# One kernel, three layers: who loads the first row list, where the first weights stand, and which engine makes the late rows' low parts

## The chip, the cores and the metric

The kernel runs on one core of a Trainium2 chip. The core has TensorE (PE, matmuls), VectorE (DVE), ScalarE (ACT), GpSimd (POOL) and SyncE (SP). DMAs are issued from the queues of SP, ACT and POOL; each queue is worked off in order. The metric is the device time of one execution in microseconds (us); three runs before the change gave 816.40, 819.06 and 818.17, median 818.17.

## The reference, cut to what matters

```python
scores = (q @ k.T) / 8                      # batch 4, 8 heads, 576 rows, head size 64
masks: heads 0-3 a local band of 32, heads 4-7 causal rows with equal position mod 32
x = softmax(where(mask, scores, -1e9)) @ v  # -> x: 2304 rows of 512
logits = x @ w_gate; e = argmax(logits)     # one of 8 experts for each row
gate = softmax(logits)[e]; eom = sigmoid((x @ w_output_gate)[e])
y = gate * eom * (relu(x @ w1[e]) @ w2[e])  # 512 -> 1024 -> 512, by expert
h = relu(y @ w_in); out = (h * h) @ w_out   # 512 -> 2048 -> 512
```

## The kernel before, in words

Three stages follow one another. Attention works batch by batch through units: a score product, softmax, a transposition, the product with v (`unit`, `unit2`, `unit3`). When all units that 128 rows need are done, `gates` makes the row tile `xr` of these rows: a product `rw` turns x over and gives the gate logits beside it, `lg` sums the logits, and SP stores the rows to the table `x_d` in DRAM. There are 18 such tiles in four groups (4, 5, 4 and 5 tiles). After a group `route` finds each row's expert (`mx`, `d`, `oh`) and its place in the expert's list (a product `rk`, then `posi`), and POOL scatters the row numbers into `tab_d`, one indirect DMA for each tile.

Second stage: the experts, largest first, 416 rows for the first. The rows of an expert are gathered from `x_d` by its list. All products are made in three parts: an operand is split into a high part (`hw`, `xh`, `xa`; ACT) and a low part (`lw`, `xl`, `xb`; a subtraction), and high x high, high x low and low x high are summed in PSUM (`mm3`). Third stage: the dense layers, on products of smaller blocks.

The place of the change is the end of attention. After group 2 (tiles 9 to 12) `largest` picks the expert that the first 13 tiles fill most, `e0`. `early_load` then loads its list `ix` from `tab_d`, two pieces of its first weights (`r`, 512 KB each) and gathers its rows (`win`, four blocks of up to 128). `first_rows` turns the first 208 of them over on PE (`wt`) and copies the others into two accumulators `lr`. The rows of the last five tiles (13 to 17) are not gathered: `late_rows` multiplies their parts `xa` and `xb` by 0/1 matrices `pm`, which put each row at its place in `lr`. Then comes the first product `h` of the expert.

A scheduler with modelled times decides the order on each engine, within the order of the program for each tile's data; `tc.issue_after` sets an instruction behind another one. Queues are first in, first out, so an instruction that waits holds up all behind it on its engine. Tile buffers: `xr` has four (`XRB`), so tile 17 takes the buffer of tile 13 after its store and its `xa` and `xb`; `raw`, `wh` and `wl` hold the weights. Names at work: L491 `xb`, L516 `ix`, L520 `win`, L534 and L538 `e0` and `r`, L587 and L596 `wt` and `lr`, L622 `lr` from `pm`, L703 the scatters, L915 and L919 `hw` and `lw`.

Of the kernel before, what the change touches and what calls it, by code (L numbers as in the profile page):

```python
# [7 lines left out]
F32 = mybir.dt.float32  # L8
# [5 lines left out]
ALU = mybir.AluOpType  # L14
# [6 lines left out]
P = 128  # L21
# [39 lines left out]
HB = 8  # L61

MG = [(3, 3), (3, 3), (3, 3)]
LPOOL = (13, 14, 15, 16, 17)
DS = 6
LN = 6
FILL = (2, 3)
PMB = 5
LWP = 0

# [61 lines left out]
def moe_kernel(ctx, tc, q, k, v, wg, wog, w1, w2, w_in64, w_out64, consts, out, dbg=None):  # L132
# [335 lines left out]
    def gates():  # L468
        while gq and needs(gq[0][1]) <= done:
            g, t = gq.pop(0)  # L470
            t0, t1 = GROUPS[g]
            if t == t0:
                xrs[g] = wk.tile([P, 5, 2 * E], F32, name=f"lg{g}", tag="lg", bufs=2), []
            lg, rows = xrs[g]
            xr = wk.tile([P, KD, W], F32, name=f"xr{t}", tag="xr", bufs=XRB)
            col = t * P % (2 * S)
            for kh in range(2):
                ps = pss.tile([P, 2, W], F32, name=f"rw{t}_{kh}", tag=TAILT.get((t, kh), "tp"))
                for kk in range(2):
                    kd = kh * 2 + kk  # L480
                    nc.tensor.matmul(ps[:, kk, :], xT[:, kd, col : col + P], igw[:, kd, :], start=True, stop=True)  # L481
                evac(xr[:, 2 * kh : 2 * kh + 2, :], ps)
            nc.vector.tensor_reduce(
                lg[:, t - t0, :], xr[:, :, P:].rearrange("p k c -> p c k"), axis=AX.X, op=ALU.add
            )
            rows.append(xr)
            if t >= LATE:
                parts[t] = xa, xb = [wk.tile([P, KD, P], F32R, name=f"x{i}{t}", tag="xp", bufs=XPB) for i in "ab"]
                nc.scalar.activation(xa, xr[:, :, :P], AF.Copy)
                eng = nc.gpsimd if t in LPOOL else nc.vector  # L490
                eng.tensor_tensor(xb, xr[:, :, :P], xa.bitcast(F32), op=ALU.subtract)  # L491
            stq(x_d[1 + t * P : 1 + (t + 1) * P, :], xr[:, :, :P])
            if t == t1 - 1:
                route(g, list(range(t0, t1)), lg, rows)
                if t1 == LATE:
                    lead["do"] = largest
                elif t0 >= LATE:
                    late_rows(t0, t1, rows)

    def stq(dst, src):  # L500
        nc.sync.dma_start(dst.rearrange("p (k c) -> p k c", c=P), src)
# [8 lines left out]

    tab_e = tab_d.rearrange("(e r) o -> e (r o)", e=E)

    def rows_of(k, reg):
        ix = const.tile([P, NW], I32, name=f"ix{k}")
        nw = (CAPS[k] + P - 1) // P
        nc.sync.dma_start(ix[:, :nw], tab_e[bass.ds(reg, 1), : nw * P].rearrange("e (c p) -> p (e c)", p=P))  # L516
        return ix

    def gather(out_, ix, n=1 + NT):
# [7 lines left out]
    def win_get(k, r, ix, n=1 + NT):  # L527
        m = min(P, CAPS[k] - r)
        wins[k, r // P] = w = early[0].tile([P, KD, P], F32, name=f"win{k}_{r}", tag="win", bufs=4)
        lead["win"] = gather(w[:m].rearrange("p k c -> p (k c)"), ix[:m, r // P : r // P + 1], n)  # L530

    def early_load():
        e0 = lead["e0"]
        oreg[0] = nc.values_load(e0[0:1, :], engines=[ET.SP], min_val=0, max_val=E - 1)  # L534
        lead["ix"] = rows_of(0, oreg[0])
        for c in range(2):
            raw = early[0].tile([P, KD, UC], F32, name=f"r0_{c}", tag="raw", bufs=2)
            nc.sync.dma_start(  # L538
                raw, w1[bass.ds(oreg[0], 1), :, c * UC : (c + 1) * UC].rearrange("e (a p) f -> p (e a) f", p=P)
            )  # L540
            eraw["w1", 0, c] = raw

        for r in range(0, CAPS[0], P):
            win_get(0, r, lead["ix"], 1 + LATE * P)

    def largest():

# [26 lines left out]
    def first_rows():  # L574

        xh = early[0].tile([P, KD, CAPS[0]], F32R, name="xh0", tag="xh")
        xl = early[0].tile([P, KD, CAPS[0]], F32R, name="xl0", tag="xl")
        xsp[0] = (xh, xl)
        acc["p"] = [pss.tile([P, 2, NL], F32, name=f"lr{h}", tag="pt") for h in range(2)]
        for t in range((CAPS[0] + P - 1) // P):  # L580
            R = min(P, CAPS[0] - t * P)
            w = wins[0, t]
            c = max(0, min(R, C0 - t * P))
            if c:
                ps = pss.tile([P, KD, P], F32, name=f"wt0_{t}", tag=("o", "os")[t % 2], bufs=1)
                for a in range(KD):
                    nc.tensor.transpose(ps[:, a, :c], w[:c, a, :], ident[:c, :c])  # L587
                cs = slice(t * P, t * P + c)
                nc.scalar.activation(xh[:, :, cs], ps[:, :, :c], AF.Copy)
                with tc.issue_after(lead["pm"].ins):  # L590
                    nc.vector.tensor_tensor(xl[:, :, cs], ps[:, :, :c], xh[:, :, cs].bitcast(F32), op=ALU.subtract)
            if c < R:
                cs = slice(t * P + c - C0, t * P + R - C0)
                with tc.issue_after(lead["rk"].ins) if t in FILL else nullcontext():
                    for a in range(KD):
                        nc.tensor.matmul(  # L596
                            acc["p"][a // 2][:, a % 2, cs],
                            w[:R, a, :],
                            ident[:R, c:R],
                            start=(t == C0 // P and a % 2 == 0),  # L600
                            stop=False,
                        )

    def late_rows(t0, t1, rows):
        rel = wk.tile([P, 5], F32, name=f"rel{t0}", tag="rel")
        nc.vector.tensor_scalar(rel[:, : t1 - t0], posi[:, t0:t1], lead["base"], None, op0=ALU.subtract)
        pms = []
        for t in range(t0, t1):
            pm = wk.tile([P, NL], F32R, name=f"pm{t}", tag="pm", bufs=PMB)
            lead["pm"] = nc.vector.tensor_scalar(  # L610
                pm, cst[:, C_IO : C_IO + NL], rel[:, t - t0 : t - t0 + 1], None, op0=ALU.is_equal
            )
            pms.append((t, pm))
        if t0 == LATE:
            first_rows()
        xh, xl = xsp[0]
        for h in range(2):
            ps = acc["p"][h]
            for t, pm in pms:
                for a in range(2):  # L620
                    for x in range(2):
                        nc.tensor.matmul(  # L622
                            ps[:, a, :],
                            parts[t][x][:, 2 * h + a, :],
                            pm,
                            start=False,
                            stop=(t == NTILE - 1 and a == x == 1),
                        )
            if t1 == NTILE:
                to = (slice(None), slice(2 * h, 2 * h + 2), slice(C0, CAPS[0]))  # L630
                nc.scalar.activation(xh[to], ps, AF.Copy)
                lead["last"] = nc.vector.tensor_tensor(xl[to], ps, xh[to].bitcast(F32), op=ALU.subtract)  # L632
# [94 lines left out]
    for b in range(B):  # L727
        t = tiles[b]
        tn = transposes(b + 1, tiles[b + 1]) if b + 1 < B else iter(())
        for n, ku in enumerate(ORDER[b].split()):  # L730
            next(tg, None)
            kind, u = ku[0], int(ku[1:])
            q2.append((b, t, kind, u) + unit(b, t, kind, u))
            drain(D2, D3)
            if b == B - 1 and n >= LN and "do" in lead:
                lead.pop("do")()
                lead["ok"] = 1
            if b == B - 1 and not early and all(a[0] == b for a in q2 + q3):
                front.close()
                early.append(  # L740
                    bulk.enter_context(tc.tile_pool(name="early", bufs=1, side="right", reuse_waits="tile"))
                )
            if scq and nun[0] >= scq[0][0] and (b < B - 1 or "ok" in lead):
                with tc.issue_after(last_ev["p"].ins):
                    scq.pop(0)[1]()
            if n >= (5 if b == 0 else 1):
                next(tn, None)
                if b == 0:
                    next(tn, None)
        for _ in tn:  # L750
            pass
        tg = iter(())
        if b + 2 < B:
            tiles[b + 2] = load(b + 2)
# [112 lines left out]
    def prep_unit(u):  # L867
# [43 lines left out]
        pool, nb = (raws, 2) if nwh[0] % WB < 2 else (mp, WB - 2)  # L911
        hi = pool.tile(shp, F32R, name="h" + nm, tag="wh", bufs=nb)
        first = u in eraw
        with tc.issue_after(last_ev["s"].ins) if first else nullcontext():
            nc.scalar.activation(hi, raw, AF.Copy)  # L915
        lo = pool.tile(shp, F32R, name="l" + nm, tag="wl", bufs=nb)
        eng = nc.gpsimd if first and LWP else nc.vector
# [472 lines left out]
```

## Time and profile before

| | us |
|---|---|
| median of three runs | 818.17 |
| the profiled execution | 815.72 |
| its span in the trace | 813.9 |
| PE busy | 763.5 (94%) |
| DVE busy | 553.9 (68%) |
| ACT busy | 493.3 (61%) |
| POOL busy | 216.8 (27%) |

The page gives the busy time of each engine, the span in 40 slices of 20.3 us, and the chain that ended last: for each piece of work what released it. The trace behind it is read by timelines (instructions in order, with the idle time before them and what ended it), by stretches (windows) and by tiles. Times below count from the span's start. An SP or POOL row of a DMA is its issue; the transfer lands later.

### The profile page before, as it was taken

Reading aid. Unit: us, or ns where it says so; the run is one execution under the profiler, and the core shown is the slowest. Engines: PE = TensorE matmul, PEld = TensorE weight load, DVE = VectorE, ACT = ScalarE, POOL = GpSimd, SP = SyncE. Lnnn points to the kernel's source line nnn. Section 1 sums busy time; section 2 is a strip of 40 time slices with the busy share of each in tenths; the row PEclk is TensorE's granted clock in tenths of the full one; section 3 lists DMA queues with packets and bytes.
Section 4 is the critical chain, followed back from the end, with each engine's and each line's share of the span. In section 5 each row is a group of like instructions: output and inputs, shape, how many; then the busy total and the mean of one; then the engine's idle time right before and its main releaser. Section 6 shows DMA issues by size and latency. Waiting matters only on the chain.

```text
span 813.9 us, 14424 instructions
## 1 busy us (share of the span) xinstructions
PE 763.5 (94%) x5139; PEld 704.9 (87%) x5139; DVE 553.9 (68%) x1109; ACT 493.3 (61%) x1197; POOL 216.8 (27%) x210
## 2 busy tenths in 40 slices
PE   4999799599999999999989999999999999999993
PEld 3988789599999999999978888888889988888893
DVE  4778578565467578779889777787654687566442
ACT  2878588524455465656677676766655586556542
POOL 7223133537065764431133121004000003000002
PEclk9999989779999999999999999999999999999998
DMA  8987801629679999876554633524232235223002
GB/s 175 201 178 136 189 21 54 191 63 333 202 188 267 196 303 283 298 258 210 172 195 147 218 128 123 175 91 149 91 118 77 76 105 182 72 87 102 1 1 81
DMA packets 106691, 124.85 MB, mean 153 GB/s; under 512 B 42801, under 2 KB 77137, under 8 KB 106610
## 3 DMA queue, kind: packets, MB, share of 16 engines
q1 hardware_dynamic: 97026, 100.77, 43.6%
q0 software_dynamic: 8096, 22.63, 8.6%
q8 instruction: 42, 0.69, 0.4%
q10 hardware_dynamic: 1488, 0.44, 0.3%
q14 instruction: 39, 0.32, 0.2%
HBM read 101.70 MB, written 22.12 MB: 152 GB/s over the span
## 4 chain that ended last, share of the span: by engine, by line
PE 55%; issue 17%; DMA 9%; DVE 7%; ACT 6%; POOL 4%; SPq 1%; POOLq 0%; ACTq 0%; DVEq 0%
DMA s0wo<-in_moe_w_out_dram 4%; PE o L935 4%; PE h L935 4%; PE o L936 4%; PE o L937 4%; PE y L935 4%; PE y L936 3%; PE h L936 3%; PE y L937 3%; PE h L937 3%; PE rw L481 2%; DMA ks<-in_k_dram 1%; DMA rw<-in_moe_w_dram 1%; POOL win L520 1%; PE lr L622 1%
## 5 line engine op out<-in xcount | busy, mean ns | idle before, releaser
L935 PE MATMUL o<-hwo,gh 128*128 128x512 f32 x288 | 114.2, 397 | 3.8 <-ACT gh L1063 3.8
L936 PE MATMUL o<-lwo,gh 128*128 128x512 f32 x288 | 113.4, 394 | 0.0
L919 DVE TENSOR_TENSOR lw<-rw,hw 128x1024 fp32r<-128x1024 f32 x62 | 78.2, 1262 | 43.2 <-ACT hw L915 42.6
L1149 ACT ACTIVATE rl<-rl 128x384 f32<-128x384 f32 x96 | 49.5, 519 | 94.9 <-DVE rl L1147 94.8
L915 ACT ACTIVATE hw<-rw 128x1024 fp32r<-128x1024 f32 x62 | 65.9, 1062 | 65.2 <-PE h L936 44.9
L1176 POOL DMA_INDIRECT out_dram<-ob,idx x18 | 20.6, 1147 | 275.5 <-ACT ob L1175 271.0
L1064 DVE TENSOR_TENSOR gl<-rl,gh 128x384 fp32r<-128x384 f32 x96 | 56.8, 593 | 44.3 <-ACT gh L1063 43.2
L937 PE MATMUL o<-hwo,gl 128*128 128x512 f32 x288 | 83.6, 396 | 2.0 <-DVE gl L1064 2.0
L935 PE MATMUL h<-xh,hw 128*128 128x416 f32 (+7 forms) x256 | 81.0, 316 | 1.6 <-DVE hl L1035 1.5
L937 PE MATMUL h<-xh,lw 128*128 128x416 f32 (+7 forms) x256 | 79.5, 310 | 0.0
L936 PE MATMUL h<-xl,hw 128*128 128x416 f32 (+7 forms) x256 | 79.5, 310 | 0.0
L936 PE MATMUL y<-hl,hw 128*128 128x416 f32 (+7 forms) x256 | 77.1, 310 | 0.0
L937 PE MATMUL y<-hh,lw 128*128 128x416 f32 (+7 forms) x256 | 76.6, 310 | 0.0
L935 PE MATMUL y<-hh,hw 128*128 128x416 f32 (+7 forms) x256 | 68.0, 311 | 0.4 <-ACT hh L1034 0.4
L935 PEld LDWEIGHTS o<-hwo,gh 128*128 128x128 f32 x288 | 54.0, 188 | 15.5 <-ACT gh L1063 6.3
L937 PEld LDWEIGHTS o<-hwo,gl 128*128 128x128 f32 x288 | 53.6, 188 | 12.8 <-DVE gl L1064 3.0
L936 PEld LDWEIGHTS o<-lwo,gh 128*128 128x128 f32 x288 | 54.1, 188 | 9.0
L1063 ACT ACTIVATE gh<-rl 128x384 fp32r<-128x384 f32 x96 | 49.9, 521 | 1.8
L935 PEld LDWEIGHTS h<-xh,hw 128*128 128x128 f32 x256 | 48.1, 188 | 3.1 <-DVE hl L1035 2.9
L1150 ACT ACTIVATE rl<-rl 128x384 f32<-128x384 f32 x96 | 49.6, 519 | 1.7
L936 PEld LDWEIGHTS h<-xl,hw 128*128 128x128 f32 x256 | 48.2, 188 | 0.3 <-DVE xl L632 0.2
L936 PEld LDWEIGHTS y<-hl,hw 128*128 128x128 f32 x256 | 48.1, 188 | 0.1
(602 smaller groups left out, 2066.6 us busy)
## 6 DMA issues: line engine op xcount, KB each, us to landing
rw<-in_moe_w_dram SPq DMA_DIRECT2D x62, 512.0 KB
rwa<-ws_d SPq DMA_DIRECT2D x24, 512.0 KB
rwb<-ws_d SPq DMA_DIRECT2D x24, 384.0 KB
e6wi<-in_moe_w_in_dram SPq DMA_DIRECT2D x32, 256.0 KB
rwo<-wout_d SPq DMA_DIRECT2D x16, 512.0 KB
x_d<-xr SPq DMA_DIRECT2D x18, 256.0 KB
ws_d<-eo POOLq DMA_DIRECT2D x16, 256.0 KB, 5.1
s0wo<-in_moe_w_out_dram SPq DMA_DIRECT2D x8, 512.0 KB
```

Source lines behind the costliest of these rows:

```text
L481: nc.tensor.matmul(ps[:, kk, :], xT[:, kd, col : col + P], igw[:, kd, :], start=True, stop=True)
L520: return nc.gpsimd.indirect_dma_start(out=out_, out_offset=None, in_=x_d[:n, :], in_offset=bass.IndirectOffsetOnAxis(ap=ix, axis=0),)
L915: nc.scalar.activation(hi, raw, AF.Copy)
L919: eng.tensor_tensor(lo, raw, hi.bitcast(F32), op=ALU.subtract)
L935: nc.tensor.matmul(ps, ah, bh, start=first, stop=False)
L936: nc.tensor.matmul(ps, ah, bl_, start=False, stop=False)
L937: nc.tensor.matmul(ps, al, bh, start=False, stop=last)
L1063: nc.scalar.activation(h, x, AF.Copy)
L1064: nc.vector.tensor_tensor(l, x, h.bitcast(F32), op=ALU.subtract)
L1149: nc.scalar.activation(rl[:, :HC], src, AF.Relu)
L1150: nc.scalar.activation(rl[:, :HC], rl[:, :HC], AF.Square)
L1176: ins = nc.gpsimd.indirect_dma_start(out=out[:, :], out_offset=bass.IndirectOffsetOnAxis(ap=idx[:, gt_, 0:1], axis=0), in_=ob, in_offset=None,
```

## The change

Seven edits. (1) The list `ix` is loaded from POOL's queue, right ahead of the gathers, and no longer from SP's; e0's value is read on POOL for it. (2) The loads of `r` become `first_weights`, called behind the store of tile 15. (3) The high parts `hw` of `r` are issued behind the last `xa`. (4) All `xb` are made on DVE; that of tile 17 behind the last `pm`. (5) `LN`, the first unit of the last batch at which `largest` may run, is 4 and was 6, and up to two scatters are issued at a step of the last batch. (6) All row transpositions and copies are issued behind `rk`. (7) `late_rows` runs its loops by half, part, tile.

```diff
-LPOOL = (13, 14, 15, 16, 17)
-LN = 6
-FILL = (2, 3)
+LN = 4
@@ gates
-                nc.scalar.activation(xa, xr[:, :, :P], AF.Copy)
-                eng = nc.gpsimd if t in LPOOL else nc.vector
-                eng.tensor_tensor(xb, xr[:, :, :P], xa.bitcast(F32), op=ALU.subtract)
+                lead["xa"] = nc.scalar.activation(xa, xr[:, :, :P], AF.Copy)
+                lead["xb"] = lambda: nc.vector.tensor_tensor(xb, xr[:, :, :P], xa.bitcast(F32), op=ALU.subtract)
+                if t < NTILE - 1:
+                    lead["xb"]()
             stq(x_d[1 + t * P : 1 + (t + 1) * P, :], xr[:, :, :P])
+            if t == NTILE - 3:
+                first_weights()
@@ rows_of, early_load
-    def rows_of(k, reg):
+    def rows_of(k, reg, eng=nc.sync):
-        nc.sync.dma_start(ix[:, :nw], tab_e[bass.ds(reg, 1), : nw * P].rearrange("e (c p) -> p (e c)", p=P))
+        eng.dma_start(ix[:, :nw], tab_e[bass.ds(reg, 1), : nw * P].rearrange("e (c p) -> p (e c)", p=P))
     def early_load():
         e0 = lead["e0"]
-        oreg[0] = nc.values_load(e0[0:1, :], engines=[ET.SP], min_val=0, max_val=E - 1)
-        lead["ix"] = rows_of(0, oreg[0])
+        e0p = nc.values_load(e0[0:1, :], engines=[ET.Pool], min_val=0, max_val=E - 1)
+        lead["ix"] = rows_of(0, e0p, nc.gpsimd)
+        for r in range(0, CAPS[0], P):
+            win_get(0, r, lead["ix"], 1 + LATE * P)
+    def first_weights():
+        oreg[0] = nc.values_load(lead["e0"][0:1, :], engines=[ET.SP], min_val=0, max_val=E - 1)
         for c in range(2):
...
@@ first_rows
-                for a in range(KD):
-                    nc.tensor.transpose(ps[:, a, :c], w[:c, a, :], ident[:c, :c])
+                with tc.issue_after(lead["rk"].ins):
+                    for a in range(KD):
+                        nc.tensor.transpose(ps[:, a, :c], w[:c, a, :], ident[:c, :c])
-                with tc.issue_after(lead["rk"].ins) if t in FILL else nullcontext():
+                with tc.issue_after(lead["rk"].ins):
@@ late_rows
+        if t1 == NTILE:
+            with tc.issue_after(lead["pm"].ins):
+                lead["xb"]()
-            for t, pm in pms:
-                for a in range(2):
-                    for x in range(2):
+            for x in range(2):
+                for t, pm in pms:
+                    for a in range(2):
@@ the loop over units
-                with tc.issue_after(last_ev["p"].ins):
-                    scq.pop(0)[1]()
+                for _ in range(2 if b == B - 1 else 1):
+                    if scq and nun[0] >= scq[0][0]:
+                        with tc.issue_after(last_ev["p"].ins):
+                            scq.pop(0)[1]()
@@ prep_unit
-        with tc.issue_after(last_ev["s"].ins) if first else nullcontext():
+        with tc.issue_after(lead["xa"].ins) if first else nullcontext():
             nc.scalar.activation(hi, raw, AF.Copy)
```

POOL at attention's end, before; `tab_d<-tok_92` is a scatter (the first is tile 8's), and the waits name the semaphores of DMA queues and engines:

```order
L372 TENSOR_TENSOR pr3s_2130<-pr3s_2130,rc3s_2137 72x4x72 [waits DVE_49,PE_49,Activation_49]
L372 TENSOR_TENSOR pr3s_2194<-pr3s_2194,rc3s_2201 72x4x72 [waits DVE_49,PE_49,Activation_49]
L372 TENSOR_TENSOR pr3s_2224<-pr3s_2224,rc3s_2231 72x4x72 [waits DVE_49,PE_49,Activation_49]
L703 DMA tab_d<-tok_92,posi 18432x1 [waits DMASW0_49]
L703 DMA tab_d<-tok_92,posi 18432x1 [waits DMASW1_49,DVE_49]
...
L703 DMA tab_d<-tok_92,posi 18432x1 [waits DMASW4_49]
L520 DMA win_0_2405<-x_d,ix_2399 128x512 [waits DMAHW4_49,DMAHW3_49,DMAHW5_49,DMAHW2_49,DMAHW6_49,DMAHW1_49,DMAHW7_49,DMAHW0_49,DMASW5_49]
...
L520 DMA win_384_2411<-x_d,ix_2399 32x512 [waits DMASW0_49]
L491 TENSOR_TENSOR xb_2482<-xr_2471,xa_2481 128x512 [waits DVE_49,Activation_49]
```

The same place now:

```order
L370 TENSOR_TENSOR pr3s_2130<-pr3s_2130,rc3s_2137 72x4x72 [waits DVE_49,PE_49,Activation_49]
L713 DMA tab_d<-tok_92,posi 18432x1 [waits DMASW0_49]
L370 TENSOR_TENSOR pr3s_2212<-pr3s_2212,rc3s_2219 72x4x72 [waits DVE_49,PE_49,Activation_49]
L370 TENSOR_TENSOR pr3s_2244<-pr3s_2244,rc3s_2251 72x4x72 [waits DVE_49,PE_49,Activation_49]
L713 DMA tab_d<-tok_92,posi 18432x1 [waits DMASW1_49,DVE_49]
...
L713 DMA tab_d<-tok_92,posi 18432x1 [waits DMASW4_49]
L536 TENSOR_LOAD e_2196 [waits DVE_49]
...
L517 DMA ix_2281<-tab_d 128x4x1 [waits DMASW5_49,DMASW4_49]
L521 DMA win_0_2283<-x_d,ix_2281 128x512 [waits DMAHW3_49,DMAHW4_49,DMAHW2_49,DMAHW5_49,DMAHW1_49,DMAHW6_49,DMAHW0_49,DMAHW7_49,DMASW6_49,DMASW5_49]
...
L521 DMA win_384_2289<-x_d,ix_2281 32x512 [waits DMASW1_49]
L713 DMA tab_d<-tok_92,posi 18432x1 [waits DMASW2_49,DVE_49]
```

The list stands between the last scatter of group 2 and the gathers, `xb` is gone, and tile 8's scatter moved ahead of two `pr3s`.

SP behind the store of tile 12, before (`r0_0` and `r0_1` are `r`):

```order
L501 DMA x_d_82<-xr12_2072 512x1x128 [waits DMAHW3_49,DVE_49,Activation_49]
L534 TENSOR_LOAD e0_2260 [waits DVE_49]
L534 ISA x2
L516 ISA
L516 DMA ix0_2399<-tab_d_83 128x4x1 [waits DMAHW4_49,DMASW4_49]
L538 ISA
L538 DMA r0_0_2401<-in_moe_w1_dram 128x4x256 [waits DMAHW5_49,PE_49]
L538 ISA
L538 DMA r0_1_2403<-in_moe_w1_dram 128x4x256 [waits DMAHW6_49]
L501 DMA x_d_82<-xr13_2471 512x1x128 [waits DMAHW7_49,DVE_49,Activation_49]
```

And now:

```order
L502 DMA x_d_82<-xr12_2072 512x1x128 [waits DMAHW3_49,DVE_49,Activation_49]
L543 TENSOR_LOAD e0_2196 [waits DVE_49]
L543 ISA x2
L546 ISA
L546 DMA r0_0_2554<-in_moe_w1_dram 128x4x256 [waits DMAHW4_49,PE_49]
L546 ISA
L546 DMA r0_1_2556<-in_moe_w1_dram 128x4x256 [waits DMAHW5_49]
L502 DMA x_d_82<-xr13_2467 512x1x128 [waits DMAHW6_49,DVE_49,Activation_49]
```

Only the list's two rows are gone from SP; `r` still stands behind tile 12's store and ahead of tile 13's.

## Rows read from the trace of the kernel before

**Rows 1.** The page, 40 slices: PE busy and granted clock, in tenths.

```profile
PE   4999799599999999999989999999999999999993
PEclk9999989779999999999999999999999999999998
```

**Rows 2.** PE timeline, end of the late products: start us, us, what.

```profile
173.62 0.28 PE L622 MATMUL lr<-pm,xb 128*128 128x208 f32 x1
173.73 0.37 PE L935 MATMUL h<-xh,hw 128*128 128x416 f32 x1
```

**Rows 3.** PE timeline, 149 to 168 us; idle time before it in brackets.

```profile
149.32 2.23 PE L481 MATMUL rw<-igw,xT 128*128 128x144 f32 x16 [0.53 <-DVE xT L270]
157.15 1.08 PE L587 MATMUL wt<-cst,win 128*128 128x128 f32 x4 [5.61 <-DMA win<-x_d,ix]
...
158.99 1.86 PE L596 MATMUL lr<-cst,win 128*128 128x48 f32 x8
163.10 0.22 PE L655 MATMUL rk<-oh,cstb 128*128 128x40 bf16 x1 [2.26 <-DVE oh L652]
...
163.53 3.92 PE L596 MATMUL lr<-cst,win 128*128 128x128 f32 x16
...
167.43 0.52 PE L622 MATMUL lr<-pm,xa 128*128 128x208 f32 x1
```

**Rows 4.** The chain that ended last, 142 to 151 us: start, us, what.

```profile
141.95 6.18 DMA tab_d<-tok,posi
148.15 2.16 DMA ix<-tab_d
```

**Rows 5.** SP's queue, issues, 148 to 159 us.

```profile
148.82 0.97 SPq L538 DMA_DIRECT2D r<-in_moe_w_dram  x2
149.91 8.54 SPq L501 DMA_DIRECT2D x_d<-xr  x5
```

**Rows 6.** POOL timeline, 131 to 163 us.

```profile
131.03 0.66 POOL L372 TENSOR_TENSOR pr3s<-pr3s,rc3s 72x288 f32<-72x288 f32 x1 [2.64 <-DVE lg L483]
...
151.39 0.99 POOL L520 DMA_INDIRECT win<-x_d,ix  x1 [8.21 <-issue]
...
155.21 0.88 POOL L520 DMA_INDIRECT win<-x_d,ix  x1 [0.30 <-issue]
156.11 6.17 POOL L491 TENSOR_TENSOR xb<-xr,xa 128x512 fp32r<-128x512 f32 x5
```

**Rows 7.** ACT timeline, the first split of r.

```profile
153.43 1.06 ACT L915 ACTIVATE hw<-r 128x1024 fp32r<-128x1024 f32 x1 [4.78 <-DMA r<-in_moe_w_dram]
```

**Rows 8.** DVE timeline, routing of the last five tiles.

```profile
157.43 0.46 DVE L270 COPY xr<-rw 128x288 f32<-128x288 f32 x1 [6.37 <-POOL xb L491]
...
158.28 0.20 DVE L638 TENSOR_REDUCE mx<-lg 128x5 f32<-128x40 f32 x1
158.51 3.83 DVE L640 TENSOR_TENSOR d<-lg,mx 128x40 f32<-128x40 f32 x1
...
164.37 1.31 DVE L610 TENSOR_SCALAR pm<-cst,rel 128x208 fp32r<-128x208 f32 x5
```

**Rows 9.** Tile ix, SP: ns min/median/max, first and last start us.

```profile
L516 SPq MOVE ix<-tab_d x8: 29/29/38, 141.5 to 320.9; - x8
```

**Rows 10.** DVE timeline, low parts of r.

```profile
166.60 2.34 DVE L919 TENSOR_TENSOR lw<-r,hw 128x1024 fp32r<-128x1024 f32 x2
```

**Rows 11.** Tile tab_d: scatters from issue to landing.

```profile
DMA to landing us min/median/max: 2.8/5.8/12.9
```

**Rows 12.** Windows: us, busy of PE, PEld, DVE, ACT, POOL, clock, DMA, GB/s.

```profile
150.00:155.00 5.00, 1.54 (x13) 1.33 (x11) 0.46 (x1) 1.13 (x2) 2.90 (x3) 0.91 1.05 287
...
165.00:170.00 5.00, 5.00 (x24) 4.71 (x24) 3.94 (x7) 0.00 (x0) 4.01 (x4) 0.50 0.10 27
```

**Rows 13.** The page's DMA issues: KB each, median us to landing.

```profile
idx<-idx_d POOLq DMA_DIRECT2D x1, 18.0 KB, 6.9
```

**Rows 14.** Tile win: gathers from issue to landing.

```profile
DMA to landing us min/median/max: 3.3/5.7/8.7
```

More of the change, by code (lines that the diff above doesn't have):

```diff
@@ L541, in early_load @@
             eraw["w1", 0, c] = raw
-        for r in range(0, CAPS[0], P):
-            win_get(0, r, lead["ix"], 1 + LATE * P)
     def largest():
```

## The prediction

> **What bounds the kernel now.** I read the slices of the page first. TensorE (PE) is near nine tenths or more in most of them; one slice in the middle, the eighth, falls to 5 while the granted clock sinks to 7 in it and in the next [rows 1]. That slice lies at 142 to 163 us, attention's end, where the first expert's rows are fetched. After it PE is full to the last slices, so I take a microsecond saved here as a microsecond of the end, and a time in this stage is told by one event: the first matmul of the first expert, h, at 173.73 us [rows 2].
>
> Second, PE's own timeline [rows 3]. The last routing products rw begin at 149.32 and end at 151.55. Then PE idles 5.61 us for the gathered rows (win). From 157.15 to 160.85 it turns the first two blocks over and copies a part of the second into the sums (wt, first lr): 3.70 us. Then it idles 2.26 us for oh, VectorE's one-hot of the last five tiles, and ranks it (rk, 0.43 us). The other blocks (lr from win) take 163.53 to 167.38, 3.85 us, and the 40 products with the late tiles (lr from pm) 167.43 to 173.73, 6.30 us. So two chains meet on PE: rows, then oh; the later one is oh.
>
> Third, what each chain waits for. Rows: the last scatter of row numbers is issued at 141.95 and has landed 6.18 us later; the list is loaded (ix) in 2.16 us [rows 4]; SP issues it at 148.15, and the weights r and five x_d stores stand behind it [rows 5]; GpSimd (POOL) starts the first gather at 151.39 [rows 6], 1.08 us after the list landed at 150.31; the block is on PE 5.76 us after that [rows 3]. oh: ScalarE (ACT) sits 4.78 us waiting for the late weights, and copies of late rows stand behind that in its queue [rows 7]; VectorE (DVE) waits 6.37 us for POOL's xb to free a buffer, copies at 157.43, and its subtraction d then takes 3.83 us beside xb instead of 0.20 us, as mx ahead of it took on the same few numbers [rows 8]. POOL's five xb run from 156.11 to 162.28, and d ends just behind them, at 162.34 [rows 6, 8].
>
> **The change part by part.** *Weights, weight splits, xb (the oh chain).* In the order SP no longer holds the list, so r leaves at about 141.5, when SP had set the list's address, for which it needs the same e0 [rows 9], and the stores behind it leave as their rows are ready. ACT's splits of r move behind the last xa, so no late row waits for it. Four xb go to DVE before the routing, one behind pm. A DVE subtraction on twice as many elements is 1.17 us (2.34 for two) [rows 10], so one xb is about 0.6 us by that row, the four together 2.4 us. I bound that at 0 (all beside waits for PE, which DVE has there) and 2.4. The buffer that tile 17 takes over is then free, and its store gone, before the product ends at 151.55; its copy comes at about 152, where before it was 157.43: 5.4 us earlier, and d costs 0.2 in place of 3.83, so 3.6 more. pm, done at 165.68 [rows 8], would be done at 165.68 - 5.4 - 3.6 = 156.7, at the latest 159.1 with all xb in front. PE needs pm only after all rows from win, far later. Behind pm DVE now has the last xb and r's two lw before the first blocks' xl: 156.7 + 0.6 + 2.3 = 159.6, about when PE has turned the first block over, so xl loses nothing. On POOL the last five scatters follow the gathers some 7 us earlier; nobody waits for them sooner. The oh chain is off the path, and none of its 9.0 us counts by itself.
>
> *What is late next: the list on POOL.* The rows chain now sets PE alone, and here the change has costs.
> - Scatter. Its landing gates the list as before. r now runs beside it, where before SP stood waiting. All scatters land in 2.8 to 12.9 us [rows 11]; this one in 6.18. Ends: -3.4 and +6.7 us. r's 1 MB at the 287 GB/s of the full stretch [rows 12] is through in 3.7 us, by about 145, before the old landing, so I take +0.7.
> - List transfer. Before, 2.16 us through SP. In the trace no list goes through POOL. The nearest rows: 2.8, the fastest scatter (128 pieces) [rows 11], and 6.9, the table idx with 2,304 pieces of 8 bytes [rows 13]. The list is 512 pieces of 4 bytes; on the line between the two that is 2.8 + 384/2176 x 4.1 = 3.5 us, and I take it. Ends: 2.16 and 6.9.
> - List to gather. Before 1.08 us, with eight further semaphores named behind the list's; now the list's is named last, and I take 0.3, the gap between two gathers. Ends 0.3 and 1.08.
> - Gather to PE: 5.76 kept (x_d and later weights still load the queues). Ends 3.3 and 8.7, all gathers [rows 14].
> - Rows on PE: 3.70 + 3.85 in one piece now, since rk is done before, at the low clock: 7.55. The fourth gather starts 3.8 us after the first, before its turn on PE 5.7 us after the first block.
> - Late products: the same 40, ordered by half and part, so 6.30 if the clock returns as far behind their start as before. The last of them, at the full clock, start 0.11 us apart [rows 2]; at the half clock that is 0.22: ends 40 x 0.11 = 4.4 and 40 x 0.22 = 8.8.
>
> The sum: 148.15 + 0.7 + 3.5 + 0.3 + 5.76 + 7.55 + 6.30 = 172.3, against 173.73: 1.4 us gained. The count (cntp) moves behind the products for 0.05 us, nothing.
>
> *The Trainium skill on the list.* On the rows a POOL transfer costs more than SP's (2.8 and up against 2.16). The Trainium skill, DMA: Bandwidth & Descriptors, section Latency and other measured facts, puts the first byte at some 0.6 us by hardware descriptors and 1 us by GpSimd's: only 0.4 apart. By it the list would take an estimated 2.56 us and h start at 171.3, 2.4 us gained.
>
> *LN, two scatters a step.* Only one scatter moves in POOL's order, tile 8's, ahead of two products pr3s. It takes 1 us where POOL idled 2.64 us before the first of them [rows 6]; if that cover were gone, pr3s would be 1 us later, a small loss. The last scatter still waits for the ranks on DVE, so it isn't earlier. *Transposes behind rk* cost nothing: rk would come at about 154, before the first block at 158.4.
>
> **Rivals.**
> *1. The clock returns earlier.* PE's row work is now one unbroken run into the late products. If the clock rises before these, they take 4.4 instead of 6.3: gain 3.3 us. Against it: before, PE worked from 163.53 without a gap and was still at a granted 0.50, 1.2 GHz, up to 170 [rows 3, 12]. The Trainium skill, TensorE: Matmul & The Clock Gate, Part 1, says that sustained activity releases the throttle; by that rule the late products would run at 2.4 GHz. The row work of before did not do it, so this stays the lesser case.
> *2. The transfers are quick.* List 2.8 and gather 4.0: 1.4 + 0.7 + 1.8 = 3.9 us gained. For it: stores and r are gone from the queues earlier. Against: the later weights move up behind them too.
> *3. The list is as slow as idx:* 6.9, so 1.4 - 3.4 = 2.0 us lost.
> *4. Slower: r beside the last scatter.* Both use the same DMA engines at 142 to 145 us. At the slowest scatter's 12.9 the list could not be asked for before 154.85, 6.0 later than in the sum: 4.6 us lost. It decides from a landing at 148.85 + 1.4 = 150.25 on. Against it: r is done by about 145.
> *5. It doesn't do what it says.* The order has the weights behind x_d of tile 12, not of tile 15. That makes nothing by itself; the oh chain could stay last only if d were 8 us later than I have it.
>
> **How the numbers follow.** The profiled execution took 815.72 us, its span 813.9 and 1.8 around it; the median shown is 818.17, 2.45 higher. 815.72 - 1.4 = 814.3, on the median's scale 816.8. A measurement of this kernel tells about 0.3%, 2.45 us, from no change. Chances: forecast, 0 to 2.4 us gained, 0.45, its own range 815.8 to 818.2; rival 1 0.20 (814.9); rival 2 0.14 (814.3); rival 3 0.10 (820.2, within 0.3%); rival 4 0.11 (822.8). Rival 5 is in the forecast's range. Faster 0.34, same 0.55, slower 0.11. The ends of the costs added up reach about 7 us gained and more than 10 lost; leaving out the outer 2 in 10 I take 813.0 to 819.8.
>
> **What would show it.** Right: SP's stores of tiles 13 to 17 start as their rows are ready; d about 0.2 us, no wait on xb; pm done near 157; ix on POOL issued near 149 and landing 3.5 us later; PE's wait before wt put down to the gather, and none between the first lr and the next; h near 172.3. Wrong: a scatter landing after 150; a list landing more than 5 us after its issue; rk or pm still the last wait before lr; the clock back before the first late product; or h earlier and the end not.

## The result and the profile after

| | before | after |
|---|---|---|
| median, runs made side by side (us) | 819.29 (8 runs) | 824.06 (8 runs, 822.29 to 827.88) |
| ratio, 95% interval | | 1.0065 [1.0037, 1.0093] |
| profiled execution, its span (us) | 815.72, 813.9 | 825.59, 823.8 |
| last scatter's issue to the first h (us) | 141.95 to 173.73: 31.78 | 143.66 to 182.61: 38.95 |
| first h to the end of the span (us) | 640.2 | 641.2 |

The changed kernel is slower by 0.65%, some 4.8 us by the medians. The forecast was 816.8 within 813.0 to 819.8, so it was wrong in sign and outside its range; what happened is rival 4, and its price, 4.6 us lost, is near the 4.8 of the medians. One profiled execution differs from another by some us: in this one the last scatter leaves 1.71 us later than before, and the first scatter of all (71.14 against 69.22) is as late already, long ahead of anything that was moved. So times below are counted from the last scatter's issue. From there to h the stage takes 7.2 us longer; that lies within what the interval allows (3.0 to 7.6), but above the medians' 4.8, and behind h this execution took 1.0 us longer.

The page's slices first. The eighth slice of PE, 144 to 165 us, fell from 5 to 4 and the ninth from 9 to 7 [rows 1]: the stage is longer.

```profile
PE   4899799479999999999989999999999999999994
PEclk9999989769999999999999999999999999999997
```

SP's queue, where r now leaves just ahead of the last scatter's issue at 143.66, and no longer behind the list [rows 5]:

```profile
143.25 1.03 SPq L546 DMA_DIRECT2D r<-in_moe_w_dram  x2
146.24 14.67 SPq L502 DMA_DIRECT2D x_d<-xr  x5
```

POOL's timeline from the last scatter to the first gather [rows 4, 6]; the bracket is the idle time ahead and what ended it:

```profile
143.66 1.19 POOL L713 DMA_INDIRECT tab_d<-tok,posi  x1 [0.30 <-issue]
159.49 0.81 POOL L517 DMA_DIRECT2D ix<-tab_d  x1 [14.64 <-DMA tab_d<-tok,posi]
162.36 1.01 POOL L521 DMA_INDIRECT win<-x_d,ix  x1 [2.06 <-DMA ix<-tab_d]
```

The list waits for the last scatter: 15.83 us from its issue to the list's, where it was 6.20. From issue to landing the last two scatters took 7.4 and 15.5 us, by the tile's answer, and the list itself 2.6 us:

```profile
DMA to landing us min/median/max: 7.4/11.4/15.5
...
DMA to landing us min/median/max: 2.6/2.6/2.6
```

Why so late shows in the windows (busy times of PE, PEld, DVE, ACT, POOL; granted clock; busy share of the DMA engines; GB/s). In the 8 us behind r's issue the DMA engines are busy for 0.91 and then 0.43 of the time and move only 21 to 24 GB/s, and then 352:

```profile
144.00:148.00 4.00, 3.76 (x53) 3.21 (x52) 3.80 (x13) 3.36 (x12) 0.84 (x1) 1.00 0.91 21
148.00:152.00 4.00, 3.33 (x45) 3.05 (x44) 3.07 (x8) 2.17 (x7) 0.00 (x0) 1.00 0.43 24
152.00:156.00 4.00, 1.35 (x11) 1.13 (x10) 0.46 (x1) 0.95 (x2) 0.00 (x0) 1.00 1.10 352
```

r doesn't run through at 287 GB/s as it did in the full stretch of before [rows 12]: beside the scatters it creeps, and the last scatter lands at about 159.2, some 3 us behind the stretch at 352 GB/s. PE's timeline [rows 2, 3]:

```profile
151.12 2.23 PE L479 MATMUL rw<-igw,xT 128*128 128x144 f32 x16 [0.67 <-DVE xT L268]
162.49 0.21 PE L665 MATMUL rk<-oh,cstb 128*128 128x40 bf16 x1 [9.14 <-DVE oh L662]
...
169.16 1.86 PE L593 MATMUL wt<-cst,win 128*128 128x128 f32 x8 [6.17 <-DMA win<-x_d,ix]
170.81 5.54 PE L602 MATMUL lr<-cst,win 128*128 128x48 f32 x24
176.29 2.46 PE L632 MATMUL lr<-pm,xa 128*128 128x208 f32 x10
...
182.61 0.44 PE L947 MATMUL h<-xh,hw 128*128 128x416 f32 x1
```

The wait ahead of wt is now for the gather, as forecast, and the 24 lr run without a gap; but all of it comes late. On DVE [rows 8, 10] d is cheap, xb is 0.68 us, and the copy of tile 17's rows has a new wait: not for xb, but for the store of tile 13, which SP issued behind r at 146.24 and which is awaited up to 159.88:

```profile
159.88 0.46 DVE L268 COPY xr<-rw 128x288 f32<-128x288 f32 x1 [7.01 <-DMA x_d<-xr]
...
161.53 0.20 DVE L650 TENSOR_TENSOR d<-lg,mx 128x40 f32<-128x40 f32 x1
...
163.75 1.49 DVE L616 TENSOR_SCALAR pm<-cst,rel 128x208 fp32r<-128x208 f32 x5
165.17 0.68 DVE L488 TENSOR_TENSOR xb<-xr,xa 128x512 fp32r<-128x512 f32 x1
```

### The profile page after: what moved, and what is told of

Its sections match the earlier page's. It is cut to its first block, busy times and chain, and to the rows that moved or that the text cites. A ratio compares the mean times of both kernels' runs of the same rounds, so it can differ in the third digit from the quotient of the medians.

```text
span 823.8 us, 14431 instructions
## 1 busy us (share of the span) xinstructions
PE 763.3 (93%) x5139; PEld 704.1 (85%) x5139; DVE 554.7 (67%) x1114; ACT 493.6 (60%) x1197; POOL 209.2 (25%) x206
```

## Experiments

Theory T1: r beside the scatters makes the last scatter late, and by that the list, the gather and h. The rival, T2 in the expectations, has the loss on another part of the change; T3 comes up with e. Ten kernels were run, each profiled once and timed beside the kernel before. All times but the ratio are from the last scatter's issue, in the profiled execution. Behind h the profiled executions took 638.6 to 643.2 us, which is as large a spread as the losses and gains in the stage; so the times tell what happened in the stage, and only the ratio tells what it was worth.

| kernel | list's issue | wt | first h | ratio to before, 95% |
|---|---|---|---|---|
| before | 6.20 | 15.20 | 31.78 | 1 |
| after | 15.83 | 25.50 | 38.95 | 1.0065 [1.0037, 1.0093] |
| after, r late (a) | 7.55 | 16.63 | 31.75 | 1.0000 [0.9977, 1.0022] |
| before, r early (b) | 15.39 | 21.90 | 35.19 | 1.0062 [1.0040, 1.0085] |
| after, list on SP, r behind it (c) | 6.38 | 16.02 | 30.05 | 0.9975 [0.9954, 0.9996] |
| after, half of r early (d) | 15.72 | 25.76 | 39.02 | 1.0087 [1.0058, 1.0116] |
| c, r behind the last store (e) | 6.31 | 15.09 | 31.58 | 0.9970 [0.9938, 1.0002] |
| c, added matmuls (f) | 6.59 | 20.72 | 28.87 | 0.9961 [0.9933, 0.9990] |
| before, xb on DVE (g) | 6.30 | 15.63 | 31.17 | 0.9978 [0.9944, 1.0012] |
| after, 1/16 of r early (i) | 8.28 | 20.76 | 35.07 | 1.0019 [0.9988, 1.0049] |
| c, fewer added matmuls (j) | 5.57 | 19.73 | 27.89 | 0.9959 [0.9926, 0.9992] |
| e, fewer added matmuls (m) | 5.96 | 27.38 | 35.54 | 0.9934 [0.9901, 0.9967] |

**a: r taken away from the scatters.**

```diff
             if t == NTILE - 3:
-                first_weights()
+                with tc.issue_after(lead["st"].ins):   # st: tile 15's store
+                    first_weights()
...
```

> The changed kernel, with the loads of r truly behind tile 15's store on SP. Theory 1 (r beside the scatters: 1 MB of loads and four scatters of 4-byte elements hold each other up, so the last scatter lands 15.5 us after its issue and the list waits): the last scatter of group 2 lands in 6 to 8 us, the store of tile 13 no longer holds tile 17's buffer, h starts within 2 us of the kernel before, and the time is at the kernel before's or up to 2 us under it (ratio 0.997 to 1.001). Theory 2 (the list on GpSimd's queue, and the low parts on VectorE, cost by themselves): the time stays with the changed kernel, ratio 1.004 to 1.008.

The harm is gone: the list is issued 7.55 us behind the last scatter instead of 15.83, and the ratio is 1.0000. So is the forecast gain: h stands where it stood before. A loss by another part would have stayed. The stores of tiles 13 to 15 now lie beside the scatters alone; the window from 145 to 153 moves 68 GB/s, and the list comes 1.35 us later than before. POOL's list, and the window:

```profile
152.91 0.81 POOL L518 DMA_DIRECT2D ix<-tab_d  x1 [6.38 <-DMA tab_d<-tok,posi]
```

```profile
145.00:153.00 8.00, 7.09 (x101) 6.09 (x97) 7.21 (x21) 6.13 (x21) 1.32 (x3) 1.00 0.29 68
```

**b: the kernel before with r alone moved ahead of the list.**

```diff
-        lead["ix"] = rows_of(0, oreg[0])
         for c in range(2):
...
+        with tc.issue_after(lead["r"].ins):
+            lead["ix"] = rows_of(0, oreg[0])
```

> The kernel before, with only r moved ahead of the list on SP (list on SP, low parts on GpSimd, all else as before). Theory 1: the last scatter lands in 12 us or more instead of 6.2, the list is asked for as much later, and the time is 5 to 9 us over the kernel before (ratio 1.006 to 1.011). Theory 2: nothing of the list's queue has changed and r is merely earlier, so the ratio is 0.998 to 1.002.

This one edit brings a ratio like that of the whole change, with the list on SP's queue and xb on POOL as before. The last scatter's landing and SP's list behind it:

```profile
DMA to landing us min/median/max: 15.4/15.4/15.4
```

```profile
158.89 0.37 SPq L516 DMA_DIRECT2D ix<-tab_d  x1
```

The order on PE is not as before, though: the first wt now stands ahead of the last rw, which waited behind it.

```profile
165.40 0.45 PE L588 MATMUL wt<-cst,win 128*128 128x128 f32 x1 [15.07 <-DMA win<-x_d,ix]
165.64 4.00 PE L481 MATMUL rw<-igw,xT 128*128 128x144 f32 x16
```

In its stage h is 3.4 us late, less than after's 7.2. The gather, with fewer transfers beside it (156 GB/s from 162 to 166, where after's had 333 from 162 to 169), was on PE after 3.55 us instead of 6.80; the rw in between cost time, and the late products, right behind that longer run of work, took 4.54 us at the full clock instead of 6.32. So b shows by itself what r does to the scatter and the list; how much of its loss in time comes from the order on PE is not shown.

**c: the list on SP again, r behind it.**

```diff
-        e0p = nc.values_load(e0[0:1, :], engines=[ET.Pool], min_val=0, max_val=E - 1)
-        lead["ix"] = rows_of(0, e0p, nc.gpsimd)
+        e0p = nc.values_load(e0[0:1, :], engines=[ET.SP], min_val=0, max_val=E - 1)
+        lead["ix"] = rows_of(0, e0p)
...
-                first_weights()
+                with tc.issue_after(lead["ld"].ins):   # ld: the list
+                    first_weights()
```

> The changed kernel, with the list back on SP and r behind it, as before; the other edits stay (splits of r behind the last high parts, low parts on VectorE, order of products, scatters). Both theories: the scatter lands in about 6 us and the list about 2.2 us later. Theory 1, which holds the other edits harmless: oh is ready early, PE has no second gap in the rows, h starts 2 to 3 us earlier than before, ratio 0.996 to 0.999. Theory 2: the low parts on VectorE cost, ratio 1.002 or more.

SP waits for the scatters again, and neither r nor a late store can leave before: the window of the 8 us behind the last scatter moves 3 GB/s, and the list is issued 6.38 us behind the scatter, as before. With the other edits kept, h comes 1.7 us sooner than before, short of the 2 to 3 expected; that it is near the 1.4 of the forecast is in part chance, as the list goes another way here. (This execution came to its last scatter 10.9 us later than that of before, by something ahead of the stage.) SP's list, POOL's first gather, PE's first h, and the window:

```profile
159.23 0.43 SPq L518 DMA_DIRECT2D ix<-tab_d  x1
```

```profile
162.49 0.99 POOL L522 DMA_INDIRECT win<-x_d,ix  x1 [8.44 <-issue]
```

```profile
182.90 0.44 PE L948 MATMUL h<-xh,hw 128*128 128x416 f32 x1
```

```profile
153.00:161.00 8.00, 7.08 (x95) 6.15 (x93) 7.06 (x20) 5.66 (x19) 1.05 (x1) 1.00 0.09 3
```

**d: half of r early; i: a sixteenth.** In d the second piece, in i all but 16 partitions of the first piece (64 KB) go behind tile 15's store.

```diff
-                first_weights()
+                first_weights([0])                     # d: piece 0; i: partitions 0 to 15 of it
+                with tc.issue_after(lead["st"].ins):
+                    first_weights([1])                 # d: piece 1; i: all the rest
```

> The changed kernel, with one piece of r (512 KB) early and the other behind tile 15's store. Theory 1, as a matter of dose: the last scatter lands in 8 to 13 us, between the full r's 15.5 and 6.2, and the time lies between a_r_late and the changed kernel (ratio 1.000 to 1.005). If any load beside the scatters does the full harm: 15 us and ratio 1.006. Theory 2: ratio 1.004 to 1.008, whatever the landing.

> The changed kernel with only 16 partitions of the first piece of r (64 KB of 1 MB) at r's early place beside the scatters; the rest behind tile 15's store, as in the version that ran level with the kernel before. Theory of the dose (the scatters lose time to the bytes or packets of r beside them): with a sixteenth of them the last scatter lands 7 to 9 us after its issue, ratio 0.999 to 1.002. Rival (half of r did the whole harm, so any load beside the scatters does, up to a fixed stall): landing 13 to 16 us, ratio 1.005 to 1.010.

With half of r early the harm is as great as with all of it: 22 GB/s from 144 to 152, and a landing after 15.4 us, against the expectation by dose. But SP issued the other half at 151.19, while the scatter was still on its way, so in the end all of r lay beside it; that half of r alone would do the same isn't shown. A sixteenth does little to the scatter, which frees the list after 8.28 us, 0.7 more than with none (a), against the expectation that any load does it all. So it depends on how much of r lies there; what lies between wasn't tried. SP's second half and POOL's list in d:

```profile
151.19 2.09 SPq L549 DMA_DIRECT2D r<-in_moe_w_dram  x1
```

```profile
159.69 0.81 POOL L519 DMA_DIRECT2D ix<-tab_d  x1 [14.54 <-DMA tab_d<-tok,posi]
```

In i the rest of r then fell on the list: the same list of 512 pieces took 5.8 us from issue to landing (2.7 in a, 2.6 in after). The profiled h was 3.3 us late; the ratio, 1.0019, doesn't exclude no change. POOL in i, and the list's landing:

```profile
152.14 0.81 POOL L519 DMA_DIRECT2D ix<-tab_d  x1 [7.10 <-DMA tab_d<-tok,posi]
158.25 3.89 POOL L523 DMA_INDIRECT win<-x_d,ix  x1 [5.30 <-DMA x_d<-xr]
```

```profile
DMA to landing us min/median/max: 5.8/5.8/5.8
```

**e: r behind the last store.** On c:

```diff
-            if t == NTILE - 3:
-                with tc.issue_after(lead["ld"].ins):
+            if t == NTILE - 1:
+                with tc.issue_after(lead["st"].ins):
                     first_weights()
```

> The changed kernel with the list back on SP, the stores of tiles 13 to 17 behind the list, and the two pieces of r behind the last of these stores (tile 17) instead of behind the list. The scatters stay undisturbed, as with the list on SP. Theory T1 (what costs the time is traffic that lies beside a stage's small transfers, so the gather too is slowed by it): the first window, which landed 6.4 us after its issue beside r and the stores, lands 1 to 2 us sooner, because 1 MB of its neighbours has gone behind; ratio to the kernel before 0.994 to 0.998. Rival T3 (only the 4-byte scatters are sensitive; the gather's 6.4 us are its own or the stores'): first window as late as with r behind the list, ratio 0.996 to 1.000. In both the landing of the last scatter is 6 to 7 us after its issue.

The first block is on PE 5.52 us after its gather's issue instead of 6.38, the way T1 said but short of its 1 to 2 us; the blocks behind it are slower (the third landed after 8.0 us, the fourth after 9.1), PE waits 2.28 us for the second, and h is 1.5 us behind c's. The interval holds both expectations; it settles nothing.

**g: the kernel before with xb on DVE.**

```diff
-LPOOL = (13, 14, 15, 16, 17)
+LPOOL = ()
```

> The kernel before with one edit: the low parts xb of tiles 13 to 17 on VectorE instead of GpSimd. List, weights and order on TensorE as before. Theory: this edit alone carries what the change gains on the rows' side: the logits' difference d no longer waits 3.83 us, the ranks come 3 to 4 us sooner, but the windows now decide, so that the first h comes 1 to 2.5 us sooner; ratio 0.997 to 0.999. Rival: the rows' work is not on the path at all, ratio 0.999 to 1.001; or VectorE, which has 3.4 us more to do, becomes late, ratio over 1.001.

d falls from 3.83 to 0.20 us, but DVE now waits 5.79 us for ACT's xa, which stands behind the splits of r (edit 3 isn't in this kernel), and PE's rank matmul still waits for the one-hot, 0.30 us. The ranks come 1.9 us earlier in the stage, but the clock comes back later into the late products, which take 7.61 us instead of 6.30, and h is only 0.6 us earlier, short of the 1 to 2.5 expected; the timed ratio doesn't tell it from no change. d and PE's rank matmul:

```profile
159.75 0.20 DVE L640 TENSOR_TENSOR d<-lg,mx 128x40 f32<-128x40 f32 x1
```

```profile
161.68 0.22 PE L655 MATMUL rk<-oh,cstb 128*128 128x40 bf16 x1 [0.30 <-DVE oh L652]
```

**f, j, m: TensorE kept at work.** Matmuls of a constant by itself, whose result nobody reads, ahead of rk and behind it: 28 and 20 (f), 14 and 12 (j on c, m on e).

```diff
+    def warm(nm, n, behind):
+        ps = pss.tile([P, KD, P], F32, name=f"warm{nm}", tag="os", bufs=1)
+        with tc.issue_after(behind.ins):
+            for i in range(n):
+                lead["warm"] = nc.tensor.matmul(ps[:, i % KD, :], ident, ident, start=True, stop=True)
```

> The changed kernel with the list on SP and r behind it, and 48 matmuls of 128x128 f32 added on TensorE whose result nobody reads: 28 behind the last rw, 20 behind the rank matmuls, so that TensorE is not idle while the list and the window are on their way. Theory of the clock (rival 1 of the prediction, the clock returns earlier): the granted clock, 0.50 from 168 to 179 with the list on SP, stays at 1.00; the 24 lr take about 3.2 us instead of 5.54 and the 40 late products about 4.5 instead of 6.6, as they did where the rows' work ran right ahead of them; the first h comes 3 to 4.5 us sooner, ratio 0.991 to 0.995. Against it: if the clock falls all the same, or what follows h waits for something else (weights of the next stretch), the ratio is 0.996 to 1.000; if the added work itself delays the window's transposes, 1.000 to 1.004.

> The version with list on SP, r behind it and added matmuls on TensorE, with 14 instead of 28 of them (3.2 us, 56 passes having taken 6.42) ahead of the ranks and 12 instead of 20 (2.75 us, 40 passes having taken 4.71) behind them, so that they end when the first window lands and hold up neither ranks nor window. Theory of the clock: it stays at 1.00, the first h comes 27.5 to 28.5 us after the last scatter's issue (28.9 with the long run of added matmuls, 30.1 without any), ratio to the kernel before 0.993 to 0.997. Against it: the shorter run leaves a pause long enough for the clock to fall, then h comes at 30 us and the ratio is that without added matmuls, 0.9975.

> The same short run of added matmuls on the version with the two pieces of r behind tile 17's store. Theory: the first window lands 0.9 us sooner than with r ahead of the stores (5.5 instead of 6.4 us), but r's late landing now decides, since lw ended only at 170.8 us there, 27.7 us after the last scatter's issue; first h 27.5 to 29 us after it, ratio 0.993 to 0.998, not better than with r behind the list. Rival: the gather was what decided, first h under 27.5 us, ratio under 0.993.

f was expected to bring h 3 to 4.5 us ahead of c and brought 1.2, and its ratio, 0.9961, is in the range of the case against it, though its interval reaches into both. At the full clock the rows take 3.60 us instead of c's 7.44 and the 40 late products 4.55 instead of 6.59, as said, 5.9 us in all; but the added work was too long (6.42 and 4.71 us) and ended at about 164, so that wt came 20.72 us behind the scatter instead of 16.02, 4.7 us lost. j, with half of it, has h and ratio in the ranges expected. From 148 us on its clock is 1.00, and its late products take 4.56 us; PE and a window of j, then the same work's window in c, at 0.50:

```profile
143.10 0.47 PE L417 MATMUL o3s<-ptp,vsp 128*64 128x72 f32 x8 [2.68 <-ACT ptp L272]
...
152.12 2.23 PE L479 MATMUL rw<-igw,xT 128*128 128x144 f32 x16 [0.67 <-DVE xT L268]
154.19 3.29 PE L618 MATMUL warma<-cst 128*128 128x128 f32 x28
...
157.71 2.92 PE L618 MATMUL warmb<-cst 128*128 128x128 f32 x24
...
164.07 1.37 PE L642 MATMUL lr<-pm,xa 128*128 128x208 f32 x10
...
168.63 0.36 PE L957 MATMUL h<-xh,hw 128*128 128x416 f32 x1
```

```profile
160.00:168.00 8.00, 8.00 (x73) 7.87 (x72) 4.36 (x6) 1.55 (x3) 5.15 (x4) 1.00 0.67 225
```

```profile
170.00:178.00 8.00, 7.74 (x36) 7.46 (x37) 2.44 (x4) 1.04 (x2) 3.92 (x4) 0.50 0.98 256
```

The Trainium skill, TensorE: Matmul & The Clock Gate, Part 1, says that activity releases the throttle; j agrees, 1.00 with the added work and 0.50 without. j's h is not a clean figure, though. In its profiled execution PE paused 2.68 us in attention, behind the last scatter's issue (the first line above; the clock was 0.63 from 144 to 148), so its last rw starts 11.4 us behind the scatter, where c's and f's start after 7.5. The expectation had no such pause, so that h fell in its range is in part chance. j's ratio and c's come from different batches, and their intervals overlap, so the 2.2 us between their h are seen in single traces alone. m has the best ratio, 0.9934 [0.9901, 0.9967], but its profiled execution had the same pause, of 2.72 us, the clock near half from 148 to 156, and its last rw only 17.4 us behind the scatter; so its h says nothing of the edit, and whether m is better than j is open. What the pause is, isn't known. c, f, j and m are faster than the kernel before by their whole intervals, m by the most.

## Why the prediction was wrong

The step that failed is the first cost of the list's chain, the scatter: "r's 1 MB at the 287 GB/s of the full stretch [rows 12] is through in 3.7 us, by about 145, before the old landing, so I take +0.7". r was not through by 145; in the 8 us from 144 the queues moved 22 GB/s. The list was asked for 15.83 us after the scatter's issue, 8.9 us later than the 6.9 in the sum. The rate was taken from a stretch in which r lay beside gathers and stores, not beside scatters. That r does this is shown both ways, by a (taken away, the list is issued after 7.55 us) and by b (added alone, after 15.39). That SP's wait for the list had kept the queues quiet in the kernel before, and that this was worth keeping, is shown by c; the prediction saw that r would run beside the scatter "where before SP stood waiting", and priced it by bytes.

The trace of before held the warning, in a row that the prediction used as an end of its range only. The scatter that took 12.9 us [rows 11] is that of 74.56, and in the 8 us behind it the next batch's loads moved 55 GB/s, with the DMA engines busy for 0.54 of the time. The scatter's landing and that window of the kernel before:

```profile
DMA to landing us min/median/max: 12.9/12.9/12.9
```

```profile
75.00:83.00 8.00, 6.86 (x84) 5.97 (x82) 4.35 (x14) 4.80 (x17) 1.52 (x3) 1.00 0.54 55
```

That is a meeting of loads and scatters too, and it was the nearest row, though that trace doesn't part the one's slowness from the other's. Rival 4 named its price (4.6 us) and the landing from which it decides, but got 0.11, on the argument that failed. The landing was 15.5 us, not the 12.9 it took; with 15.5 its sum gives 7.2 us lost, the trace's figure, so that 4.6 is near the medians' 4.8 is in part luck.

The other terms, from the trace of after:
- *Oh chain.* d 0.20 us, as said; xb 0.68 against 0.6. But pm, said for 156.7 to 159.1, ended at 165.24, which is 21.6 us behind the last scatter where the forecast had 14.8 to 17.2: tile 17's buffer waited 7.01 us for the store of tile 13, which crept beside the scatter. That was off the path, as the ranks came 6.2 us ahead of the window. In a, without r, pm ended 14.7 us behind the scatter, and in both d and the ranks are no longer last.
- *List on POOL and gather's issue.* 2.87 us from the one issue to the other; the sum had 3.5 + 0.3, and the kernel before 3.24 through SP. The estimate for the list's transfer from the Trainium skill, DMA: Bandwidth & Descriptors, Latency and other measured facts, 2.56, was close to the measured 2.6, but nothing depended on it. Rival 3 is out.
- *Gather to PE.* 6.80 against 5.76. Gathers landed in 4.9 to 6.5 us.
- *Rows on PE, late products.* 7.13 against 7.55, and 6.32 against 6.30. The clock came back inside the late products, as before, though PE worked without a gap from 169.16: it was 0.50 up to 179 and 1.00 from 181. Rival 1 came only where other work stood ahead: the added matmuls (f, j, m), or the last rw behind the first wt (b).
- *Sum.* 8.9 of the scatter, -0.9 of the list, 1.0 of the gather, -0.4 of the rows: 8.6 above the forecast's stage of 30.35 us (141.95 to 172.3), about the 38.95. But the scatter isn't all that kept the gain away. In a, with r out of its way and the list on POOL, h came after 31.75, 1.4 above the forecast: 0.65 by the list's later issue, 0.4 by the gather, 0.9 by the rows, where PE waited 1.23 us for the second block, and 0.4 by the late products, against 0.85 won on the list. c, with the list on SP, took 30.05.

## What to carry to other kernels

Before a load is moved to an earlier place, look at what small transfers lie there: a wait on a queue may be keeping the DMA engines quiet for a chain of 4-byte pieces. Price the meeting from a row where the two kinds met, not from bytes by the best rate. And with the waits in place, look at the clock of a stage of many small matmuls: the same 40 products took 4.6 instead of 6.6 us. How much of that reaches the end isn't shown, as the ratios of c, f and j overlap.

## What was not expected of the hardware

- Loads in runs of 256 numbers (r) and scatters of 4-byte pieces hold each other up both ways: r's stretch fell to 22 GB/s with the DMA engines busy for 0.67 of it, and the scatter went from 6.2 to 15.5 us. The Trainium skill, DMA: Bandwidth & Descriptors, Specifications, says that below 512 B a transfer becomes a read-modify-write. The slow 4-byte scatters would fit that; no run here varied the piece, so the cause on the chip isn't shown.
- Splitting r did not help: with half of it early and half at 151.19 the scatter landed after 15.4 us, with all of it early after 15.5. A sixteenth, the rest at 151.08, cost some 0.7 us.
- A list of 512 pieces took 2.6 to 2.7 us on POOL's queue where r wasn't beside it and 5.8 where it was. By the same page, section Issuing engines are not separate DMA queues, DMAs of all issuing engines interleave on the same DMA engines; that agrees, as r came from SP and the list from POOL.
